# Clustered attention and two expert layers on one core: mask weights and a ranking step one slot later on VectorE, TensorE's slot in another order

## The chip, the cores and the metric

The kernel runs on one core of one Trainium2 chip, as one program with one launch. The metric is the device time of the whole program in microseconds (us), lower is better. The core has five engines that run their own instruction streams and wait for one another by semaphores: TensorE (PE, matmuls and transposes), VectorE (DVE), ScalarE (ACT), GpSimd (POOL) and SyncE (SP, which issues the DMAs here).

## The reference

Three layers follow one another. Only the first is touched by the change:

```python
q_assign = np.argmax(np.einsum('bhsd,hcd->bhsc', q_n, c_n), axis=-1)
k_assign = np.argmax(np.einsum('bhsd,hcd->bhsc', k_n, c_n), axis=-1)
mask = q_assign[:, :, :, None] == k_assign[:, :, None, :]
scores = scale * np.matmul(q, k.transpose(0, 1, 3, 2))
scores = np.where(mask, scores, -1000000000.0)
scores = scores - np.max(scores, axis=-1, keepdims=True)
attn = np.exp(scores)
attn = attn / (np.sum(attn, axis=-1, keepdims=True) + 1e-09)
return np.matmul(attn, v)
```

q, k and v have 2 batches, 8 heads, 768 tokens and 64 values per head; each head has 16 cluster centres, and a query sees only the keys of its own cluster. The result goes through a layer with a rational function between two matrices (512 to 2048 to 512), and then through a layer of 8 experts with soft slots.

## The kernel before, in words

**Pairs and slots.** Attention works on pairs of heads (the two heads of a pair share the partitions), 8 pairs in all. Each pair is cut into 12 slots, so that there are 96 slots, and one loop (L692) runs over slots n. In slot n the *second pass* of slot n and the *first pass* of slot n + 10 are done (`LEAD`, L125). Below, k is n modulo 12, the place of a slot in its pair; a number in brackets is n itself.

- The first pass (`a1_mm`, L375, matmuls L383 and L384) makes the scores of 128 queries against 768 keys in PSUM. VectorE negates them and takes the minimum (`a1_neg`, L393); ScalarE takes the exponent and its sum (`a1_exp`, L401). This gives each query's largest score and sum.
- `stats` (L403) turns these into a logarithm (ACT, L409 and L410), splits it into three bf16 parts on GpSimd (L419 to L432, six steps `parts`), transposes the parts on TensorE (`rows`, L437) and puts them as extra rows under q (`place`, DVE, L444).
- The second pass (`a2_mm`, L451, matmuls L458 and L459) makes the scores with keys on the partitions and the logarithm already taken off; ScalarE takes the exponent (`a2_exp`, L463); the product with v (`a2_av`, L465, matmuls L472) adds up six slots in one PSUM bank, which ScalarE copies out (`copy`, L483) after the sixth, and GpSimd splits (`split`, L492 and L493).

**Buffers that matter.** The scores of both passes take turns in two PSUM tiles (`psS`, tag `S`, L114): within a slot the second pass has one and the first pass the other. There is one PSUM bank for the product with v, three for the small work (`m_tile`, L167), two tiles each for `neg` and `e`.

**Preparation.** `prep(p)` (L236) lists what is to be done for a later pair, three pairs ahead: each step has an offset from the slot in which the list is added (k = 8), an engine and a function. Its steps are cluster scores on TensorE (L251), scaled on ACT (L256), transposed (L266), the best cluster (`best`, DVE, L274 and L275), the first of equal clusters by a rank (`first(0)` L283, `first(1)` L285, `first(2)` L288), the one-hot rows transposed (L293) and counted (ACT, L296), `masks` (DVE, L302, L303, L304: which clusters have a key, then the tile `W` of mask weights), `nonhot` (PE, L309, which reads `W`), `signed` (ACT, L314; the second one issues four DMAs from SP), `alive` (PE, L322), `qalive` (DVE, L326), `ksplit` and `qsplit` (GpSimd, L260, L261, L333 to L335). By their offsets `first(0)` runs at k = 1, `masks` and both `nonhot` at k = 6, `signed` at k = 7 and k = 8. Pair 1 takes its slots from the tuple `PREP1` (L127), and pair 0 is prepared ahead of the loop.

**Decoding.** 32 tiles of 64-bit weights are turned into fp32 beside attention (`decode_steps`, L551): two bit operations on DVE (`bits`, L563 and L564), an exponent on ACT (L567), the mantissa and the sign on DVE (L570, L574), a product and a split on GpSimd (L579, L586, L587), and for half of them transposes and a small product on TensorE (`wphi_steps`, L601, L610, L622). A tile starts every third slot, from slot 72 on every second.

**What sets the order.** TensorE, ScalarE, VectorE and GpSimd run in the order in which the loop calls them (`manual_schedule`, L675); SP's order is left to the framework's planner. The dictionary `plan` holds for each slot and engine the steps that are due; `run(n, ...)` (L663) issues them: at the start of a slot those of SP, ACT, DVE (`D0`, `D`, `D1`, `D2`) and GpSimd, and those of TensorE (`"P"`, the small work) where the loop says so. A slot of TensorE is thus, in this order:

```python
if 0 <= n < NSL:
    a2_mm(p, k)                # second pass of slot n
    a2_exp(p, k)
if n > 0:
    a2_av(pp, pk)              # product with v of slot n - 1
if pend:
    a1_exp(*pend)              # ACT, first pass of slot n - 1
if n + LEAD < NSL:
    a1_mm(*pend)               # first pass, slot n + 10
    a1_neg(*pend)
run(n, "P")                    # small work
```

ScalarE's slot is its planned steps, `a2_exp(n)`, after every sixth product the copy, then `a1_exp` of the slot before. VectorE's slot is its planned steps and then `a1_neg`.

**After attention** the two expert layers run (L753 on); no line of them is changed.

Of the kernel before, what the change touches and what calls it, by code (L numbers as in the profile page):

```python
# [62 lines left out]
def tile_kernel(ctx, tc, qT, kT, v, cenT, cenP, consts, constsb, ab, w_in, w_out, phi, w1, w2, out, dbg=None):  # L63
# [60 lines left out]

    LEAD = 10  # L125

    PREP1 = (-9, -9, -8, -10, -7, -7, -10, -7, -6, -5, -5, -4, -4, -3, -2, -1, 0, 1, -1, 0, 1, 2, -1, 0, 2, 3)  # L127

    OPENW = 4
    ops = [[{n: att.tile([128, S], F32R, name=f"{n}_{i}_{h}") for n in ("q1", "q2", "k1", "k2")}  # L130
# [41 lines left out]
    def first_pair(r, o, f):  # L172

        hold = f["hold"]

        def nonhot_k(h):
            m = psS.tile([128, 2, 512], F32, tag="S", name="s1")
            for c in range(2):
                PE.matmul(m[64:80, c, 0:HS], hold["W"][:, 288 + 16 * h:304 + 16 * h],
                          hold["oT"][:, c * HS:(c + 1) * HS], start=True, stop=True)  # L180
            ACT.activation(o[h]["k2"][64:80, :].rearrange("p (c n) -> p c n", c=2), m[64:80, :, 0:HS], AF.Copy, scale=-BIG)

        def nonhot_q(h, c):
            m = m_tile()
            w = slice(c * HS, (c + 1) * HS)
            PE.matmul(m[64:80, 0:HS], hold["W"][:, 256 + 16 * h:272 + 16 * h], hold["oT"][:, w], start=True, stop=True)
            ACT.copy(o[h]["q2"][64:80, w], m[64:80, 0:HS])

        def q0(h):
            w = slice(0, HS)  # L190
            q1, q2 = o[h]["q1"], o[h]["q2"]
            qa = hold.pop(("qa", h, 0))
            ACT.copy(q1[:, w], qa)
            POOL.tensor_scalar(q2[0:64, w], qa[0:64, :], 1.0, 1.0, ALU.mult, ALU.mult)
            DVE.tensor_tensor(q1[64:128, w], qa[64:128, :], q1[64:128, w].bitcast(F32), ALU.subtract)

        def front():
            f["scores"](0)
            f["scores"](1)
            for h in range(2):  # L200
                f["ksplit"](h)
            idle(2)
            f["scaled"](0)
            f["scT"](0)
            f["best"](0)
            f["scaled"](1)
            f["scT"](1)
            f["best"](1)
            for i in range(3):
                f["first"](i)  # L210
            idle(12)
            f["ohT"]()
            f["count"]()
            idle(8)
            f["masks"]()

        def back():
            f["alive"](0, 0)
            f["alive"](1, 0)
            f["qalive"](0, 0)  # L220
            f["qalive"](1, 0)
            nonhot_k(0)
            q0(0)
            nonhot_q(0, 0)
            q0(1)
            nonhot_k(1)
            nonhot_q(1, 0)
            idle(4)

        rest = [(0, "P", lambda: (f["alive"](0, 1), f["alive"](1, 1))),  # L230
                (1, "D", lambda: (f["qalive"](0, 1), f["qalive"](1, 1))),
                (1, "G", lambda: (f["qsplit"](0, 1), f["qsplit"](1, 1))),
                (1, "P", lambda: (nonhot_q(0, 1), nonhot_q(1, 1)))]
        return front, back, rest

    def prep(p):  # L236
# [4 lines left out]
        hold = {}  # L241
        order = [r["q", 0], r["q", 1], r["k", 0], r["k", 1]]

        def tile_(pool, tag, shape, dt):
            hold[tag] = pool.tile(shape, dt, tag=tag, name=tag)
            return hold[tag]
# [52 lines left out]
        def masks():  # L299

            pres = tile_(s2_p, "pres", [64, 1], F32)
            DVE.memset(pres, 0.0)  # L302
            DVE.tensor_scalar(pres[0:32, :], hold["cnt"][32:64, :], 1.0, None, ALU.min)  # L303
            DVE.scalar_tensor_tensor(tile_(s2_p, "W", [64, B_ADD - B_MASK], BF16), cb[0:64, B_MASK:B_ADD], pres,  # L304
                                     cb[0:64, B_ADD:B_RANK], ALU.mult, ALU.add)

        def nonhot(c):
            m = hold["m", c] = m_tile()
            PE.matmul(m[0:64, 0:HS], hold["W"][:, 256:320], hold["oT"][:, c * HS:(c + 1) * HS], start=True, stop=True)  # L309
# [27 lines left out]
        if p == 0:  # L337
# [6 lines left out]
            (4, "A", lambda: scaled(1)),  # L344
            (4, "D0", lambda: best(0)),
            (4, "P", lambda: scT(1)),
            (5, "D0", lambda: (best(1), first(0))),
            (4, "G", lambda: ksplit(0)),
            (6, "D0", lambda: first(1)),
            (7, "D0", lambda: first(2)),  # L350
            (7, "G", lambda: ksplit(1)),
            (7, "P", ohT),
            (8, "A", count),
            (10, "D0", masks),
            (10, "P", lambda: nonhot(0)),
            (11, "A", lambda: signed(0)),
            (10, "P", lambda: nonhot(1)),
            (12, "A", lambda: signed(1)),
            (12, "P", lambda: alive(0, 0)),
            (13, "P", lambda: alive(1, 0)),  # L360
# [295 lines left out]
    NSL = 12 * NP  # L656
# [35 lines left out]
    for n in range(-LEAD, NSL + 1):  # L692
        p, k = divmod(n, 12)
# [21 lines left out]
        if 0 <= n < NSL:  # L715
            a2_mm(p, k)
            a2_exp(p, k)
        if n > 0:
            pp, pk = divmod(n - 1, 12)
            a2_av(pp, pk)  # L720
            if pk % 6 == 5:
                copy, split = a2_x(pp, pk // 6)
                copy()
                if n < NSL:
                    add(n + (1 if k else 2), [(0, "G", split)])
                else:
                    split()
        if pend:
            a1_exp(*pend)
            pend = None  # L730
        if n + LEAD < NSL:
# [4 lines left out]
            if n < 0:  # L736

                a1_mm(*divmod(n + 1 + LEAD, 12))
        run(n, "P")
        if n < -1:  # L740
            idle(2)
    DVE.tensor_scalar(ncoef, coef, -1.0, None, ALU.mult)
# [448 lines left out]
```

## Time and profile before

| what | value |
|---|---|
| median of 3 runs | 597.94 us (597.42 to 599.94) |
| profiled execution, its own time | 601.37 us |
| its span, first to last instruction | 599.6 us |
| granted TensorE clock over the span | 0.989 |
| attention's slots, and what is left | about 43 to 337 us, 337 to 600 us |
| one pair of heads in the middle of attention | 38.97 us, 12 slots |
| busy PE, DVE, ACT, POOL | 93%, 78%, 66%, 63% |

The profile is of one execution. Times in it are us from the first instruction. The page gives busy shares for the whole span; the trace behind it gives each instruction with its start, its duration and, in square brackets, how long its engine stood idle before it and what ended that. A matmul's printed duration overlaps with the next one's, so that the cost of a group on TensorE is read from starts: from its first start to the first start of what follows.

### The profile page before, as it was taken

Reading aid. Unit: us, or ns where it says so; the run is one execution under the profiler, and the core shown is the slowest. Engines: PE = TensorE matmul, PEld = TensorE weight load, DVE = VectorE, ACT = ScalarE, POOL = GpSimd, SP = SyncE. Lnnn points to the kernel's source line nnn. Section 1 sums busy time; section 2 is a strip of 40 time slices with the busy share of each in tenths; the row PEclk is TensorE's granted clock in tenths of the full one; section 3 lists DMA queues with packets and bytes.
Section 4 is the critical chain, followed back from the end, with each engine's and each line's share of the span. In section 5 each row is a group of like instructions: output and inputs, shape, how many; then the busy total and the mean of one; then the engine's idle time right before and its main releaser. Section 6 shows DMA issues by size and latency. Waiting matters only on the chain.

```text
span 599.6 us, 9906 instructions
## 1 busy us (share of the span) xinstructions
PE 557.7 (93%) x3343; PEld 344.6 (57%) x3346; DVE 468.7 (78%) x817; ACT 393.2 (66%) x713; POOL 377.4 (63%) x487
## 2 busy tenths in 40 slices
PE   8899999999989999999899989999999999978995
PEld 3465555565555655555555667776667757753363
DVE  5779788798787987988984299999899998962033
ACT  3667777787677776787686487777578767740111
POOL 8749899697996988979658365565366545611000
PEclk9989999999999999999999999999999999989999
DMA  8613563354424633244343366766477547379996
GB/s 225 230 37 116 163 192 138 110 181 159 168 89 165 200 117 123 75 137 150 125 157 125 126 224 227 266 210 215 154 270 231 197 164 276 94 293 366 420 419 257
DMA packets 37906, 113.77 MB, mean 190 GB/s; under 512 B 5216, under 2 KB 5664, under 8 KB 33248
## 3 DMA queue, kind: packets, MB, share of 16 engines
q1 hardware_dynamic: 37856, 113.14, 54.1%
q8 instruction: 26, 0.43, 0.3%
q14 instruction: 24, 0.20, 0.1%
HBM read 96.02 MB, written 15.73 MB: 186 GB/s over the span
## 4 chain that ended last, share of the span: by engine, by line
PE 47%; DVE 26%; ACT 10%; POOL 8%; issue 7%; DMA 1%; SPq 0%; DVEq 0%; POOLq 0%; ACTq 0%
DVE neg L393 5%; PE s L383 5%; PE av L472 4%; PE s L458 4%; PE h L809 3%; PE h L812 3%; PE h L810 3%; PE s L384 3%; DVE p L859 3%; PE s L459 3%; PE pb L1042 3%; PE pb L1113 2%; DVE mh L564 2%; ACT neg L401 2%; DVE p L858 2%
## 5 line engine op out<-in xcount | busy, mean ns | idle before, releaser
L393 DVE TENSOR_SCALAR_CACHE_REDUCE neg<-s 128x768 f32<-128x768 f32 x96 | 91.3, 951 | 38.3 <-ACT neg L401 26.1
L463 ACT ACTIVATE e<-s 128x768 f32<-128x768 f32 x96 | 77.5, 807 | 58.3 <-PE s L459 58.2
L401 ACT ACTIVATE neg<-neg,nv 128x768 f32<-128x768 f32 x96 | 89.4, 932 | 9.2 <-DVE neg L393 8.9
L383 PE MATMUL s<-k,q 128*128 128x384 f32 x192 | 76.5, 398 | 13.3 <-DVE neg L393 9.5
L840 POOL TENSOR_SCALAR q<-u,babs 128x512 f32<-128x512 f32 x47 | 40.3, 858 | 75.9 <-ACT u L838 75.9
L472 PE MATMUL av<-e,vt 128*64 128x384 f32 x384 | 83.2, 512 | 0.2 <-ACT e L463 0.2
L809 PE MATMUL h<-xh,w 128*128 128x512 f32 x192 | 80.7, 420 | 0.0
L383 PEld LDWEIGHTS s<-k,q 128*128 128x128 f32 x192 | 36.6, 191 | 68.3 <-DVE neg L393 26.8
L810 PE MATMUL h<-xl,w 128*128 128x512 f32 x192 | 75.9, 395 | 0.0
L458 PE MATMUL s<-q,k 128*128 128x384 f32 x192 | 73.1, 381 | 0.7 <-DVE neg L393 0.5
L842 POOL TENSOR_TENSOR q<-q,u 128x512 f32<-128x512 f32 x47 | 63.8, 1357 | 3.9
L384 PE MATMUL s<-k,q 80*128 80x384 f32 x192 | 65.5, 341 | 0.0
L459 PE MATMUL s<-q,k 128*128 128x384 f32 x192 | 64.7, 337 | 0.0
L812 PE MATMUL h<-xh,w 128*128 128x512 f32 x192 | 52.7, 396 | 0.0
L579 POOL TENSOR_TENSOR w<-mh,ex 128x512 f32<-128x512 f32 x32 | 44.3, 1383 | 10.6 <-DMA w_out<-w 5.3
L859 DVE SCALAR_TENSOR_TENSOR p<-q,p 128x512 f32<-128x512 f32 (+1 forms) x49 | 49.2, 1005 | 0.1
L849 ACT ACTIVATE r<-q,epsc 128x512 f32<-128x512 f32 (+1 forms) x49 | 33.5, 684 | 21.9 <-POOL q L842 20.6
L838 ACT ACTIVATE u<-h 128x512 f32<-128x512 f32 x47 | 27.8, 591 | 27.7 <-PE h L812 27.7
L809 PEld LDWEIGHTS h<-xh,w 128*128 128x128 f32 x192 | 36.2, 189 | 16.9 <-issue 10.3
L458 PEld LDWEIGHTS s<-q,k 128*128 128x128 f32 x192 | 36.0, 188 | 16.2 <-issue 8.3
L841 DVE TENSOR_TENSOR p<-p,h 128x512 f32<-128x512 f32 x47 | 31.8, 677 | 16.9 <-ACT p L839 16.8
L812 PEld LDWEIGHTS h<-xh,w 128*128 128x128 f32 x192 | 36.3, 189 | 8.9
(193 smaller groups left out, 1219.3 us busy)
## 6 DMA issues: line engine op xcount, KB each, us to landing
wt<-w SPq DMA_DIRECT2D x32, 1024.0 KB, 8.0
w<-w_in SPq DMA_DIRECT2D x96, 256.0 KB, 3.1
raw<-w_in SPq DMA_DIRECT2D x16, 512.0 KB, 3.6
raw<-w_out SPq DMA_DIRECT2D x16, 512.0 KB, 3.4
w_in<-w SPq DMA_DIRECT2D x16, 512.0 KB, 2.7
rawk<-kT SPq DMA_DIRECT2D x14, 384.0 KB, 4.0
rawq<-qT SPq DMA_DIRECT2D x14, 384.0 KB, 3.6
w_out<-w SPq DMA_DIRECT2D x16, 256.0 KB, 3.3
```

Source lines behind the costliest of these rows:

```text
L383: PE.matmul(ps[:, c, 0:HS], o["q1"][:, it], o["k1"][:, w], start=True, stop=False)
L384: PE.matmul(ps[:, c, 0:HS], o["q2"][0:80, it], o["k2"][0:80, w], start=False, stop=True)
L393: DVE.tensor_scalar(neg, s1s.pop((p, idx))[:, :, 0:HS], -1.0, None, ALU.mult, ALU.min, accum_out=nvs[p, half][0][:, 0, col:col + 1])
L401: ACT.activation(neg, neg, AF.Exp, scale=-1.0, bias=nv[:, 0, col:col + 1], accum_out=ssum[:, col:col + 1])
L458: PE.matmul(ps[:, h, 0:HS], o["k1"][:, jt], o["q1"][:, w], start=True, stop=False)
L459: PE.matmul(ps[:, h, 0:HS], o["k2"][:, jt], o["q2"][:, w], start=False, stop=True)
L463: ACT.activation(e, s2s.pop((p, k))[:, :, 0:HS], AF.Exp)
L472: PE.matmul(a[64 * h:64 * h + 64, 0:HS], vs[p][:, h, j, :], e[:, h, :], start=(j == 0), stop=(j == 5))
L809: PE.matmul(h, wh[:, c, :], xh[t][:, c, :], start=(c == 0), stop=False)
L810: PE.matmul(h, wh[:, c, :], xl[t][:, c, :], start=False, stop=False)
L812: PE.matmul(h, wl[:, c, :], xh[t][:, c, :], start=False, stop=(c == NCC - 1))
L859: DVE.scalar_tensor_tensor(p[:, w], q[:, w], 2.0, p[:, w], ALU.subtract, ALU.mult)
```

## The change

The step `masks` is cut in two: the memset and the minimum stay at offset 10, and the operation that makes `W` becomes a step `weights` at offset 11 (k = 7). Both `nonhot` move from offset 10 to 11 (k = 7), the first `signed` from 11 to 12 (k = 8). `first(0)` moves from offset 5 to 6 (k = 1 to k = 2), into one step with `first(1)`. `PREP1` gets one more entry, so that pair 1 has masks and weights in the same slot. In the loop the product with v, with the copy and the split that follow it, goes from behind the second pass to the end of the slot.

```diff
-    PREP1 = (-9, -9, -8, -10, -7, -7, -10, -7, -6, -5, -5, -4, -4, -3, -2, -1, 0, 1, -1, 0, 1, 2, -1, 0, 2, 3)
+    PREP1 = (-9, -9, -8, -10, -7, -7, -10, -7, -6, -5, -5, -5, -4, -4, -3, -2, -1, 0, 1, -1, 0, 1, 2, -1, 0, 2, 3)
...
             f["masks"]()
+            f["weights"]()
...
             DVE.tensor_scalar(pres[0:32, :], hold["cnt"][32:64, :], 1.0, None, ALU.min)
+
+        def weights():
+            pres = hold["pres"]
             DVE.scalar_tensor_tensor(tile_(s2_p, "W", [64, B_ADD - B_MASK], BF16), cb[0:64, B_MASK:B_ADD], pres,
                                      cb[0:64, B_ADD:B_RANK], ALU.mult, ALU.add)
...
-            (5, "D0", lambda: (best(1), first(0))),
+            (5, "D0", lambda: best(1)),
             (4, "G", lambda: ksplit(0)),
-            (6, "D0", lambda: first(1)),
+            (6, "D0", lambda: (first(0), first(1))),
...
             (10, "D0", masks),
-            (10, "P", lambda: nonhot(0)),
-            (11, "A", lambda: signed(0)),
-            (10, "P", lambda: nonhot(1)),
+            (11, "D0", weights),
+            (11, "P", lambda: nonhot(0)),
+            (12, "A", lambda: signed(0)),
+            (11, "P", lambda: nonhot(1)),
             (12, "A", lambda: signed(1)),
...
             a2_mm(p, k)
             a2_exp(p, k)
+        if pend:
+            a1_exp(*pend)
+            pend = None
+        if n + LEAD < NSL:
+            pend = divmod(n + LEAD, 12)
+            if n > 0 or n == -LEAD:
+                a1_mm(*pend)
+            a1_neg(*pend)
+            if n < 0:
+
+                a1_mm(*divmod(n + 1 + LEAD, 12))
+        run(n, "P")
         if n > 0:
+
             pp, pk = divmod(n - 1, 12)
             a2_av(pp, pk)
...
-        if pend:
-            a1_exp(*pend)
...
-        run(n, "P")
```

## Rows read from the trace of the kernel before

**Rows 1.** The page, its first part: engines over the whole span.
```profile
PE 557.7 (93%) x3343; PEld 344.6 (57%) x3346; DVE 468.7 (78%) x817; ACT 393.2 (66%) x713; POOL 377.4 (63%) x487
```
**Rows 2.** Windows (length, then busy PE, PEld, DVE, ACT, POOL): a pair; attention's end.
```profile
197.71:236.70 38.99, 37.36 (x214) 21.82 (x211) 33.00 (x62) 29.30 (x55) 33.46 (x49) 1.00 0.43 148
273.40:310.00 36.60, 33.33 (x189) 20.67 (x188) 33.85 (x57) 27.84 (x50) 26.05 (x39) 1.00 0.42 146
```
**Rows 3.** Timeline of PE, slots k = 4 to 6: start, duration, instruction, idle before.
```profile
212.13 0.45 PE L383 MATMUL s<-k,q 128*128 128x384 f32 x1
...
213.04 0.28 PE L437 MATMUL mb<-cb,stat 128*32 128x128 bf16 x2
213.25 0.44 PE L458 MATMUL s<-q,k 128*128 128x384 f32 x1
...
214.15 0.87 PE L472 MATMUL av<-e,vt 128*64 128x384 f32 x4
214.95 0.45 PE L383 MATMUL s<-k,q 128*128 128x384 f32 x1
...
215.76 0.34 PE L458 MATMUL s<-q,k 128*128 128x384 f32 x1
...
216.56 0.87 PE L472 MATMUL av<-e,vt 128*64 128x384 f32 x4
```
**Rows 4.** Timeline of GpSimd, one pair: the logarithm's parts, first and last step.
```profile
186.69 0.20 POOL L419 TENSOR_SCALAR s<-ssum 128x6 f32<-128x6 f32 x1 [3.38 <-ACT neg L401]
...
211.52 0.59 POOL L432 TENSOR_TENSOR stat<-r,stat 128x12 bf16<-128x12 f32 x1
...
225.69 0.20 POOL L419 TENSOR_SCALAR s<-ssum 128x6 f32<-128x6 f32 x1 [2.50 <-ACT neg L401]
```
**Rows 5.** Timeline of PE, the waits at k = 2, 6 and 7.
```profile
205.68 0.44 PE L383 MATMUL s<-k,q 128*128 128x384 f32 x1 [0.65 <-DVE neg L393]
...
218.83 0.51 PE L309 MATMUL mf<-oT,W 64*64 64x384 bf16 x2 [0.22 <-DVE W L304]
...
221.47 0.45 PE L383 MATMUL s<-k,q 128*128 128x384 f32 x1 [0.44 <-DVE neg L393]
222.29 0.60 PE L601 MATMUL mf<-cst,w 128*128 128x128 f32 x4
222.65 0.42 PE L458 MATMUL s<-q,k 128*128 128x384 f32 x1
```
**Rows 6.** Timeline of VectorE, k = 1 and 2, then k = 6 and 7.
```profile
202.14 0.36 DVE L283 TENSOR_TENSOR eq<-eq,cb 128x384 bf16<-128x384 bf16 x1
202.42 2.33 DVE L570 SCALAR_TENSOR_TENSOR mh<-raw,mh 128x512 f32<-128x512 uint32 x1
...
211.33 0.68 DVE L570 SCALAR_TENSOR_TENSOR mh<-raw,mh 128x512 f32<-128x512 uint32 x1
...
217.82 0.95 DVE L304 SCALAR_TENSOR_TENSOR W<-cb,pres 64x320 bf16<-64x320 bf16 x1
218.70 0.41 DVE L563 TENSOR_SCALAR ex<-raw 128x512 int32<-128x512 int32 x1
219.04 1.50 DVE L564 TENSOR_SCALAR mh<-raw 128x512 int32<-128x512 int32 x1
220.46 0.94 DVE L393 TENSOR_SCALAR_CACHE_REDUCE neg<-s 128x768 f32<-128x768 f32 x1
```
**Rows 7.** Timeline of GpSimd beside them.
```profile
201.37 0.83 POOL L260 TENSOR_SCALAR k<-rawk 128x768 fp32r<-128x768 f32 x1
202.28 1.92 POOL L261 TENSOR_TENSOR k<-rawk,k 64x768 fp32r<-64x768 f32 x1
...
218.51 1.75 POOL L579 TENSOR_TENSOR w<-mh,ex 128x512 f32<-128x512 f32 x1
```
**Rows 8.** Timeline of ScalarE, last slots with a first pass.
```profile
316.72 0.81 ACT L463 ACTIVATE e<-s 128x768 f32<-128x768 f32 x1 [0.77 <-PE s L459]
...
318.48 0.30 ACT L409 ACTIVATE l<-ssum,epsc 128x6 f32<-128x6 f32 x1
```

More of the change, by code (lines that the diff above doesn't have):

```diff
@@ L717, in tile_kernel @@
             a2_exp(p, k)
[L718 to L727, printed above, removed]
         if pend:
@@ L739, in tile_kernel @@
         run(n, "P")
+        if n > 0:
+            pp, pk = divmod(n - 1, 12)
+            a2_av(pp, pk)
+            if pk % 6 == 5:
+                copy, split = a2_x(pp, pk // 6)
+                copy()
+                if n < NSL:
+                    add(n + (1 if k else 2), [(0, "G", split)])
+                else:
+                    split()
         if n < -1:
```

## The prediction

> **What bounds the kernel now.** I read the page's busy shares first: TensorE is busy 93% of the span, VectorE 78%, GpSimd 63% [rows 1]. That is an average over stages with different limits, so I looked at the windows next. In a pair of heads in the middle of attention (38.99 us) TensorE has 37.36 us of work on record, GpSimd 33.46 and VectorE 33.00; near the end of attention VectorE has 33.85 of 36.60 [rows 2]. So TensorE leads in the middle, but two others are close, and the question is what stops it when it gets faster. The expert layers, after 337 us, are not touched; I let whatever attention gains or loses pass through whole.
>
> The timeline of TensorE shows what a slot costs, from start to start [rows 3]. A first pass between other kinds of matmul takes 0.91 us (212.13 to 213.04), a second pass 0.90 (213.25 to 214.15), the product with v 0.80. Where there is no small work, a first pass is followed directly by a second pass, and then they take 0.81 (214.95 to 215.76) and 0.80 (215.76 to 216.56): **0.20 us less as neighbours**.
>
> The timeline of GpSimd shows the second limit [rows 4]. At k = 9 its first step on the logarithm's parts waits (2.50 and 3.38 us idle) for ScalarE's exponent; from there GpSimd has work without a gap worth naming until the last of the next half's parts, at k = 4 of the next pair: 186.69 to 212.10, or 25.42 us. TensorE transposes those parts at 213.04 [rows 3], 0.93 us after they are ready. From there to the next k = 9 it is 12.65 us (213.04 to 225.69). So one pair is a **loop**: 25.42 + 0.93 + 12.65 = 39.0 us. It runs five times, from k = 9 of the first pair to k = 9 of the sixth. Only 0.93 us of it is slack.
>
> TensorE's own waits in the pair [rows 5]: at k = 2 the first pass for VectorE (0.65 us), at k = 6 the product for `nonhot` for W (0.22), at k = 7 the first pass again (0.44). That is 1.3 us together. VectorE is late at k = 2 because the mantissa takes 2.33 us, against 0.68 elsewhere, and at k = 7 because W (0.95) and the second bit operation (1.50) lie ahead of the negation, which ends at 221.40 [rows 6]. Both long operations end 0.3 to 0.6 us after a GpSimd operation that was running beside them, at 204.20 and 220.26 [rows 7].
>
> **The change, part by part.**
>
> *The order of TensorE's slot.* No instruction is added. The cycle before is second pass, v, first pass, small work; after it is second pass, first pass, small work, v. So passes are now neighbours in every slot, where before they were so only without small work. Of twelve slots one had none (k = 5). Nine of the other eleven save 0.20; the two that end with transposes of decoded weights save perhaps half, as there the first pass already took 0.82 us (221.47 to 222.29) [rows 5]. That is 9 x 0.20 + 2 x 0.1 = 2.0 us a pair. With the waits gone too, TensorE alone would need 38.99 - 2.0 - 1.3 = 35.7 us.
>
> What moves behind: the product with v itself, whose input is long there (ScalarE's exponent is what the second pass ahead of it also waits for); the copy on ScalarE, now behind `a1_exp`, and GpSimd's split, issued a slot later in any case. The one bank of the product is needed again 2.6 us of passes later, so the copy has cover. The second pass now comes 0.80 us later against the first, and with it ScalarE's exponent and everything queued behind it, the logarithm above all. At k = 9 that is in the loop, and I count it there.
>
> *Weights and `nonhot` a slot later.* One W (0.95) goes from VectorE's k = 6 to k = 7, two small matmuls with it (0.51 together), one `signed` from k = 7 to k = 8 on ScalarE. No DMA changes its slot: the four come with the second `signed`, which stays. GpSimd gets none of it; SP's order is the planner's, which I take as unchanged. What waits for W is `nonhot`, now behind the decode transposes at k = 7, with the product with v and the next second pass queued behind it.
>
> *`first(0)` a slot later.* 0.36 us [rows 6] goes from k = 1 to k = 2. At k = 1 the mantissa could then start at 202.06 instead of 202.42, while GpSimd's earlier operation (201.37 to 202.20) still runs and before the long one starts at 202.28 [rows 7]. Either it stays blocked until 204.20 and nothing changes, or it goes first, VectorE wins up to 1.6 us, and GpSimd's chain grows by up to 0.68, in the loop. Against that stands the last step on the parts, which took 0.59 against 0.20 for the first and could get 0.35 back. I take 0 between -0.35 and +0.68, since GpSimd's phase against VectorE shifts by more than the 0.22 us that decide this.
>
> The Trainium skill, page SBUF — State Buffer, section "Who interferes with whom", says that a VectorE operation with two SBUF inputs and a GpSimd operation that reads SBUF take turns, whoever issues first holding the port for its whole instruction. The trace agrees (2.33 against 0.68 us). By that rule alone the mantissa goes first and each of the five loops grows by about 0.6: 594.7 us instead of the sum below.
>
> *The loop after.* From the transposes at k = 4 to the second pass at k = 8, if nothing waits: small work 0.21, then three times v 0.80 and the joined passes 1.61, then decode transposes 0.36, `nonhot` 0.51, v 0.80: 9.1 us. The second pass there is 0.90; its exponent to the logarithm on ScalarE is 1.76 (316.72 to 318.48) [rows 8]; with 0.1 us of hand-over that makes 11.8 instead of 12.65 us. The wait that can remain is the first pass at k = 7 for the negation of k = 6: by this walk TensorE is there 6.6 us after the transposes. The negation now ends 8.36 us after them (213.04 to 221.40); without W 7.4, and if the second bit operation isn't blocked (0.41, as its neighbour, instead of 1.50) 6.3. So 0 to 0.77 us of wait, and 11.8 to 12.55 us. The slack of 0.93 goes to about 0.05, as TensorE now waits for the parts. **25.42 + 0.05 + 11.8 to 12.55 = 37.3 to 38.0 us, a gain of 1.0 to 1.7 a pair; I take 1.3.**
>
> *Sum.* Five loops: -6.5 us. Before the first pair's k = 9, and from 273 to 310 us, where VectorE is the bound at 92%, I expect little, -0.4 (0 to -1.5). At the end of the first pass's slots the logarithm decides when GpSimd can go on to the last decoded tiles, and it comes later, because the product with v now stands ahead of the second pass whose exponent is queued before it: +0.75 (0 to +0.8). Together -6.2 us. Against the profiled execution's own time that is 601.37 - 6.2 = 595.2; that execution lies 3.4 us above the median of the runs, so against 597.94 it is **591.7 us**. The first pair's and pair 1's edits change places within slots ahead of the loop: nothing either way.
>
> **Rivals.**
>
> - *GpSimd gives it back.* The mantissa goes first at k = 1 (chain +0.68) and the wait at k = 7 is the long one: 26.10 + 0.05 + 12.55 = 38.7, gain 0.3 a pair, and 597.94 - 1.5 + 0.75 = 597.2. For it: slack of 0.93 only [rows 4]. Against it: both ends must fall badly.
> - *The passes don't join.* The first pass waits for VectorE at its first matmul, as it does at k = 2 and k = 7 [rows 5], so its weights aren't ready ahead. Then the walk is about 0.6 us longer, gain 0.7 a pair, or some 595.2 with the tail.
> - *Slower: the first pass at k = 7.* `nonhot` no longer gives cover at k = 6, so TensorE arrives earlier and stands longer. If GpSimd's product runs later and keeps the second bit operation out for another 0.41 us even without W's time being won, the negation ends 8.8 us after the transposes, TensorE waits 2.1 there, and the loop is 26.10 + 0.05 + 13.9 = 40.1: 1.1 worse in five pairs, with the tail 604.2. It decides from about 8.3 us on, which is where the negation ends now; W's 0.95 must be lost again to GpSimd's turns.
> - *TensorE goes free.* If GpSimd's idle time (2.5 us at k = 9) can all be used, the pair falls to about 36 us: 597.94 - 15 + 0.75 = 583.7. Against it: the logarithm's place in the loop.
>
> **How the numbers follow.** About 0.5% (3 us) is what a measurement of this kernel can tell from no change. Forecast 0.49 (own range 588 to 594.9, by 1.7 a pair and -1.5 elsewhere at one end, 0.8 at the other), TensorE free 0.06: faster 0.55. GpSimd gives it back 0.22 and no joining 0.07, both within 3 us of 597.94 by price: same 0.29. Slower 0.16. The range 587 to 600 leaves out TensorE free and most of the slower case, about 0.2.
>
> **What would show it.** A second pass followed by a first pass 0.18 us after its last matmul's start in nearly all slots; a pair of 37.3 to 38.0 us; TensorE's transposes of the parts now waiting for GpSimd at k = 4; no wait for W; the wait at k = 2 smaller; GpSimd's idle time at k = 9 down from 2.5 us by less than a microsecond and a half. Wrong would be: a pair at 39 us or above, with a long wait of the first pass at k = 7, or a pair below 37 with no wait for the parts.

## The result and the profile after

The changed kernel takes 606.65 us (median of 4 runs, 604.78 to 607.56) beside 598.94 us for the kernel before on the same chip (4 runs): ratio **1.0133, 95% interval 1.0111 to 1.0155**. It is slower; 591.7 us was forecast.

The profiled execution took 607.56 us, its span is 605.8. The page, engines over the span and the clock in tenths by slice, answers to [rows 1]:

```profile
PE 554.1 (91%) x3343; PEld 351.1 (58%) x3346; DVE 462.3 (76%) x817; ACT 389.1 (64%) x713; POOL 376.5 (62%) x487
...
PEclk9998998999999899999899999999999999989999
```

The clock row of the kernel before:

```profile
PEclk9989999999999999999999999999999999989999
```

The work is the same, and the shares of PE, DVE, ACT and POOL are lower (that of the weight loads, PEld, is 58% instead of 57%), so time went into standing still. The added time lies in attention: the expert layers' first matmul starts at 343.90 us (337.28 before), and from there to the last matmul of that line it is 185.94 us (185.96 before). The prediction cuts its loop at k = 9, at GpSimd's first step on the logarithm's parts. GpSimd, these steps in the first, sixth and seventh pair, before and then changed:

```profile
69.77 0.20 POOL L419 TENSOR_SCALAR s<-ssum 128x6 f32<-128x6 f32 x1 [1.53 <-ACT neg L401]
...
264.40 0.20 POOL L419 TENSOR_SCALAR s<-ssum 128x6 f32<-128x6 f32 x1 [2.50 <-ACT neg L401]
...
302.07 0.26 POOL L419 TENSOR_SCALAR s<-ssum 128x6 f32<-128x6 f32 x1
```

```profile
71.27 0.20 POOL L424 TENSOR_SCALAR s<-ssum 128x6 f32<-128x6 f32 x1 [4.90 <-ACT neg L406]
...
267.63 0.20 POOL L424 TENSOR_SCALAR s<-ssum 128x6 f32<-128x6 f32 x1 [2.44 <-ACT neg L406]
...
306.44 0.26 POOL L424 TENSOR_SCALAR s<-ssum 128x6 f32<-128x6 f32 x1
```

So the 6.62 us are 1.50 ahead of the first pair's k = 9, 1.73 in the five turns of the loop, 1.14 in the turn behind them, and 2.25 from there to the expert layers, which is called the tail below.

Below, a pair is read from its first product with v to that of the next pair, a turn from k = 9 to k = 9. Windows (length, then busy PE, PEld, DVE, ACT, POOL, then the granted clock): two whole pairs and one short stretch; they answer to [rows 2].

```profile
207.27:245.58 38.31, 35.97 (x212) 22.28 (x211) 31.98 (x62) 28.57 (x55) 31.47 (x48) 1.00 0.39 131
...
87.55:127.59 40.04, 36.89 (x207) 23.01 (x207) 31.68 (x61) 28.30 (x55) 32.87 (x47) 0.96 0.45 148
...
98.15:101.56 3.41, 3.41 (x10) 2.60 (x12) 1.84 (x3) 1.72 (x3) 3.33 (x4) 0.50 0.31 86
```

Two kinds of pair, then. The first has the full clock and is 38.3 us long; the second holds a stretch of 3.41 us in which the granted clock is 0.50, the 1.2 GHz level, and is 40.0 long. Attention has four such stretches (at 53.8, 98.2, 197.1 and 296.1 us); the kernel before had none between its first pair and the expert layers (one lies ahead of them, at 30.3 us).

Timeline of TensorE (start, duration, instruction, idle before), the slots k = 3 and 4 of one pair, then k = 7 and k = 10 of a later one:

```profile
94.26 0.34 PE L463 MATMUL s<-q,k 128*128 128x384 f32 x1
94.44 0.34 PE L464 MATMUL s<-q,k 128*128 128x384 f32 x1
94.61 0.33 PE L388 MATMUL s<-k,q 128*128 128x384 f32 x1
...
97.06 0.29 PE L442 MATMUL mb<-cb,stat 128*32 128x128 bf16 x2 [1.59 <-POOL stat L437]
97.28 0.87 PE L477 MATMUL av<-e,vt 128*64 128x384 f32 x4
98.08 0.64 PE L463 MATMUL s<-q,k 128*128 128x384 f32 x1
98.52 0.52 PE L464 MATMUL s<-q,k 128*128 128x384 f32 x1
98.84 0.52 PE L463 MATMUL s<-q,k 128*128 128x384 f32 x1
99.16 0.52 PE L464 MATMUL s<-q,k 128*128 128x384 f32 x1
...
184.64 0.66 PE L606 MATMUL mf<-cst,w 128*128 128x128 f32 x4 [1.02 <-POOL w L584]
185.23 0.51 PE L313 MATMUL mf<-oT,W 64*64 64x384 bf16 x2
185.67 0.87 PE L477 MATMUL av<-e,vt 128*64 128x384 f32 x4
...
194.73 0.33 PE L326 MATMUL mf<-oT,W 64*128 64x384 bf16 x1
196.17 0.51 PE L252 MATMUL mf<-rawq,cT 64*32 64x384 f32 x2 [1.11 <-ACT sc L257]
```

Four things stand in these rows. The passes did join, in 56 of the 60 slots of pairs 1 to 5: a first pass starts 0.17 us after the second pass's last matmul (94.44 to 94.61), as in the joined slot of [rows 3]. Small work now waits, and behind it stand the product with v and the next second pass: at k = 4 the transposes wait for GpSimd's parts (1.59), at k = 7 the decoded tile's transposes for GpSimd's product of the same slot (1.02), at k = 10 the second cluster scores for ScalarE, which has to free one of the three small PSUM tiles (1.11). In the kernel before these three didn't wait in pairs 1 to 5. Now the first waits in pairs 1, 2, 3 and 5, the second in pairs 2, 3 and 5, the third in pairs 0 to 4; in pairs 1 and 4 it is the first pass that waits at k = 7, for VectorE (0.45 and 0.74). And about 1 us after two of these waits the spacing of the matmuls goes from 0.17 to 0.32 us (98.52, 98.84, 99.16): the low clock. The other two falls of the clock follow waits of the first pass for VectorE, 1.74 us up to 52.83 in pair 0 and 1.53 us up to 294.74.

Timeline of GpSimd, the loop of [rows 4] in one pair, and the product that TensorE awaits at k = 7:

```profile
94.45 0.52 POOL L424 TENSOR_SCALAR s<-ssum 128x6 f32<-128x6 f32 x1
...
96.77 0.24 POOL L437 TENSOR_TENSOR stat<-r,stat 128x12 bf16<-128x12 f32 x1
...
111.29 0.20 POOL L424 TENSOR_SCALAR s<-ssum 128x6 f32<-128x6 f32 x1 [3.58 <-ACT neg L406]
...
182.59 2.00 POOL L584 TENSOR_TENSOR w<-mh,ex 128x512 f32<-128x512 f32 x1
```

From the parts' end (97.01) to the transposes it is now 0.05 us, as predicted. From the transposes (97.06) to GpSimd's next first step (111.29), the prediction's walk from k = 4 to k = 9, it is 14.2 us here, and 13.2 to 13.8 in the pairs after it, where 11.8 to 12.55 was forecast and 12.6 to 13.1 is what the kernel before has. GpSimd stands idle for 3.58 us at the end of it; at the ends of the five turns it is 15.4 us in all, 15.1 before, so no less.

Counted over 44 to 334 us, TensorE waits 0.8 us or more 3 times in the kernel before and **18 times** in the changed one.

### The profile page after: what moved, and what is told of

Its sections match the earlier page's. It is cut to its first block, busy times and chain, and to the rows that moved or that the text cites. A ratio compares the mean times of both kernels' runs of the same rounds, so it can differ in the third digit from the quotient of the medians.

```text
span 605.8 us, 9903 instructions
## 1 busy us (share of the span) xinstructions
PE 554.1 (91%) x3343; PEld 351.1 (58%) x3346; DVE 462.3 (76%) x817; ACT 389.1 (64%) x713; POOL 376.5 (62%) x487
## 4 chain that ended last, share of the span: by engine, by line
PE 54%; DVE 17%; POOL 12%; ACT 8%; issue 6%; DMA 2%; SPq 0%; DVEq 0%; POOLq 0%; ACTq 0%
PE av L477 8%; PE s L463 5%; PE s L388 4%; PE h L815 4%; PE h L818 3%; PE h L816 3%; PE s L464 3%; PE s L389 3%; DVE p L865 3%; PE pb L1048 3%; POOL w L584 2%; DVE p L864 2%; PE pb L1119 2%; ACT e L468 2%; DVE neg L398 2%
## 5 line engine op out<-in xcount | busy, mean ns | idle before, releaser
L477 PE MATMUL av<-e,vt 128*64 128x384 f32 x384 | 85.4, 520 | 0.2 <-ACT e L468 0.2
L388 PE MATMUL s<-k,q 128*128 128x384 f32 x192 | 68.9, 359 | 11.5 <-DVE neg L398 7.6
L463 PE MATMUL s<-q,k 128*128 128x384 f32 x192 | 76.6, 399 | 0.1
L464 PE MATMUL s<-q,k 128*128 128x384 f32 x192 | 66.0, 344 | 0.0
L584 POOL TENSOR_TENSOR w<-mh,ex 128x512 f32<-128x512 f32 x32 | 43.9, 1371 | 11.8 <-DMA w_out<-w 5.3
L388 PEld LDWEIGHTS s<-k,q 128*128 128x128 f32 x192 | 37.2, 194 | 18.7 <-DVE neg L398 11.3
```

Of the source, the lines that this page charges most:

```text
L388: PE.matmul(ps[:, c, 0:HS], o["q1"][:, it], o["k1"][:, w], start=True, stop=False)
L463: PE.matmul(ps[:, h, 0:HS], o["k1"][:, jt], o["q1"][:, w], start=True, stop=False)
L464: PE.matmul(ps[:, h, 0:HS], o["k2"][:, jt], o["q2"][:, w], start=False, stop=True)
L477: PE.matmul(a[64 * h:64 * h + 64, 0:HS], vs[p][:, h, j, :], e[:, h, :], start=(j == 0), stop=(j == 5))
```

## The experiments

The expectations speak of three theories. A: the loop of the prediction stands, and the new order lengthens it because small work with waits of its own now stands in TensorE's path ahead of the product and the next second pass. B: the moved steps do it, through VectorE's and GpSimd's turns. C: the granted clock, which falls after TensorE has stood still, makes a part of the loss of its own. The kernel before ran beside each, with medians of 597.91 to 599.70 us. Where lines are quoted below, they are those of that kernel. The length of a slot is read from the last matmul of its second pass to that of the next slot.

**Which part of the change it is: e1, e2, e14, e15.** e1 is the kernel before with the new order of TensorE's slot alone:

```diff
+        if pend: a1_exp ...; a1_mm ...; a1_neg ...
+        run(n, "P")
         if n > 0: a2_av(pp, pk) ...
-        if pend: a1_exp ...; a1_mm ...; a1_neg ...
-        run(n, "P")
```

> The kernel before with only TensorE's slot in the new order (second pass, first pass, small work, product with v); weights, nonhot and first(0) stay where they were. Theory A (small work now stands ahead of the product with v, so that its waits for GpSimd and ScalarE are no longer filled): nearly the whole loss is here, 603 to 607 us, ratio 1.008 to 1.015, with waits of the small work at k = 4, 7 and 10 and drops of the granted clock in attention. Theory B (weights and nonhot one slot later are the loss, the order by itself is a gain): 590 to 595 us.

606.71 us, 1.0135 (1.0114 to 1.0156), with four stretches at the low clock between 51 and 239 us and 16 waits of 0.8 us or more. The order alone makes the whole loss, but not by the waits of the changed kernel, and the expectation was wrong on two of its three places. TensorE in one pair of e1, k = 2 and k = 6:

```profile
169.41 0.44 PE L383 MATMUL s<-k,q 128*128 128x384 f32 x1 [1.04 <-DVE neg L393]
...
181.38 0.44 PE L383 MATMUL s<-k,q 128*128 128x384 f32 x1 [1.12 <-DVE pres L302]
```

Of the small work only the scores at k = 10 wait long here (1.11), and the transposes at k = 4 and k = 7 don't. Instead the first pass waits for VectorE, at k = 2 (1.0 to 1.95, in three pairs), k = 6 (0.5 to 1.1) and k = 7 (0.4). The five turns are 39.7 to 40.0 us, the three with a low clock in them no longer than the two without. That the two totals agree within 0.1 us doesn't make it one set of waits. e2 is the rest of the change: the changed kernel with the old order.

> The kernel before with only the steps moved (weights, nonhot, signed and first(0) one slot later), TensorE's slot in the old order. Theory A: no loss, 595 to 600 us; the waits for VectorE at k = 2 and k = 7 change by a few tenths. Theory B: 603 to 607 us.

601.24 us, 1.0042 (1.0024 to 1.0059): a loss of its own, which A did not expect, and no part of the sum, for e1 already has it all. The five turns don't show it (194.3 us, 194.6 before). In the profile it lies ahead of the first pair's k = 9 (72.16 us, 69.77 before), where the clock is at 0.50 for 6.8 us instead of 3.4. Timeline of VectorE in e2, then of GpSimd, at k = 1:

```profile
165.33 0.69 DVE L575 SCALAR_TENSOR_TENSOR mh<-raw,mh 128x512 f32<-128x512 uint32 x1
```

```profile
164.66 0.83 POOL L261 TENSOR_SCALAR k<-rawk 128x768 fp32r<-128x768 f32 x1
165.57 2.15 POOL L262 TENSOR_TENSOR k<-rawk,k 64x768 fp32r<-64x768 f32 x1
```

Without the ranking step ahead of it the mantissa starts 0.24 us before GpSimd's long operation and takes 0.69 us, where it took 2.33 [rows 6]; GpSimd's takes 2.15 instead of 1.92 [rows 7], and its chain is 25.92 us instead of 25.41. The wait at k = 2 goes with it (that slot 2.97 us, 3.66 before), but at k = 7 the slot is 4.2 to 4.5 us instead of 3.36, and pairs alternate between 38.05 and 39.6 us. e14 moves only the weights, `nonhot` and the first `signed`, e15 only `first(0)`, in the kernel before; this is the edit of e15:

```diff
-            (5, "D0", lambda: (best(1), first(0))),
+            (5, "D0", lambda: best(1)),
-            (6, "D0", lambda: first(1)),
+            (6, "D0", lambda: (first(0), first(1))),
```

> The kernel before with only the mask weights, nonhot and the first signed a slot later. If the two moved steps cost 0.4% through the wait of the first pass at k = 7 for VectorE (W now stands ahead of the negation there): about 601 us, slot k = 7 at 4.2 us or more against 3.4. If they cost it through the mantissa going first at k = 1: about 598, and slot k = 7 as before.

> The kernel before with only the first ranking step moved from k = 1 to k = 2. If the mantissa goes first and lengthens GpSimd's chain: chain 25.9 us, slot k = 2 at 3.0 instead of 3.6 us, and 600 us or more. If W's move is what costs: about 598 us, the shorter wait at k = 2 paying for the longer chain.

e14: 600.29 us, 1.0042 (1.0027 to 1.0058), slot k = 7 at 4.5 us, turns 0.26 us longer than before. Timeline of VectorE in e14, k = 6 and 7; then of TensorE:

```profile
178.56 0.90 DVE L568 TENSOR_SCALAR ex<-raw 128x512 int32<-128x512 int32 x1
179.37 1.51 DVE L569 TENSOR_SCALAR mh<-raw 128x512 int32<-128x512 int32 x1
180.80 0.95 DVE L398 TENSOR_SCALAR_CACHE_REDUCE neg<-s 128x768 f32<-128x768 f32 x1
...
181.68 1.01 DVE L308 SCALAR_TENSOR_TENSOR W<-cb,pres 64x320 bf16<-64x320 bf16 x1
```

```profile
181.82 0.44 PE L388 MATMUL s<-k,q 128*128 128x384 f32 x1 [0.96 <-DVE neg L398]
```

W is gone from ahead of this negation, and still nothing is won: the first bit operation now takes 0.90 instead of 0.41 us, the second 1.51 as before [rows 6], and TensorE, which no longer stops for `nonhot` at k = 6, is there earlier and stands 0.96 us instead of 0.44 [rows 5]. The expectation had W ahead of the negation; the rows show it behind. e15: 600.09 us, 1.0018 (0.9999 to 1.0037), not clear of no change: the chain is 25.7 us, slot k = 2 is 2.97 in most pairs, and pairs lie anywhere from 37.8 to 40.4 us (the longest has a fall of the clock in it), with waits for the parts (0.52) and, at k = 6, for VectorE's minimum (1.10). Its two runs at a clock of 0.997 and 0.998 took 597.3 and 596.9 us, the eight at 0.987 to 0.992 took 599.5 to 601.5. So e14's step alone costs as much as both together, and that e15's costs anything by itself is not shown. Why the two don't add up in e2 stays open.

**Where v stands: e3, e4.** e3 is the changed kernel, e4 the kernel before, each with the product with v between the first pass and the small work (passes joined, but a wait of small work no longer holds up v):

> The changed kernel with the product with v between the first pass and the small work (second pass, first pass, v, small work): the passes stay neighbours, the small work gets back the 0.8 us of cover ahead of it. Theory A: the waits at k = 7 and k = 10 shrink by about 0.8 us each and the time goes to 592 to 600 us. Theory B: 602 to 607 us.

> The same order (second pass, first pass, v, small work) without the moved steps. Theory A: 592 to 600 us, within 0.5% of the run with the moved steps. Theory B: 588 to 594 us, faster by 1% or more than the run with the moved steps.

e3: 604.02 us, 1.0082 (1.0059 to 1.0105). e4: 609.68 us, 1.019 (1.0139 to 1.0241), five stretches at the low clock in attention. A had 592 to 600 us for both and missed both; B had e3 right by its time and missed e4. Neither does better than the kernel before, and with the old steps this order is the worst of all (at k = 2 the first pass waits 1.75 to 1.97 us in every one of pairs 0 to 5). In e3's profile pairs 0 to 4 are 38.4 to 38.8 us long, a little under the 38.98 of before, with a chain of 26.0 to 26.3. Its ten runs fall apart by the clock: two at 0.995 took 599.7 and 600.0 us, the eight at 0.984 to 0.990 took 602.8 to 605.3.

**Which wait: e5, e6, e7, e9.** All are the changed kernel. e5 takes the wait at k = 7 away by moving the decoded tile's transposes (and what follows, for the tiles begun before slot 72) a slot later, e6 the one at k = 10 by moving the second cluster scores to k = 11, e7 does both, and e9 is e7 with the last two steps of every fourth tile three slots later still:

```diff
-            return [(4, "P", tr), (5, "A", tcopy), ...
+            j = 1 if f < 12 else 0
+            return [(4 + j, "P", tr), (5 + j, "A", tcopy), ...
-            (2, "P", lambda: scores(1)),
+            (3, "P", lambda: scores(1)),
```

> The changed kernel, with the transposes of the decoded w_out tiles and what follows them one slot later (for the tiles begun before slot 72), so that TensorE at k = 7 doesn't wait for the product that GpSimd makes in the same slot. Theory A (the pair is a loop through GpSimd: logarithm's parts, transposes of the parts at k = 4, decoded tile, transposes at k = 7, exponents, next logarithm): the wait at k = 7 goes (1.0 us), the way from k = 4 to k = 9 falls from 13.2 to about 12 us, a pair to about 37.7 us, and the time to 597 to 602 us. Theory C (the clock's drops in attention are nearly all of the loss, and the waits themselves cost nothing): the same number of drops, 604 to 607 us.

> The changed kernel, with the second cluster scores one slot later (k = 11), so that they don't wait at k = 10 for ScalarE to empty the buffer of the first. Theory A: the wait at k = 10 (1.1 us) goes, but it lies beside GpSimd's chain, so a pair without a clock drop stays within 0.3 us of 38.3 to 39.1; the time falls only by what fewer clock drops give, 602 to 607 us. Theory D (the wait at k = 10 is on the path): a pair falls by 1 us, 600 to 602 us.

> The changed kernel with both moves. Theory A: pairs of 37.5 us, no more than one clock drop in attention, 594 to 600 us, so at or below the kernel before. Theory C: as many clock drops as the waits that are left cause; 600 to 604 us.

> The kernel of the two moves (transposes of the decoded tiles and second cluster scores one slot later), with the closing transposes and the sum of every fourth tile three slots later still, since the pairs that hold them took 39.9 us and the others 37.5. Theory A (loop through GpSimd, and VectorE's turns with GpSimd inside it): all pairs 37.3 to 37.8 us, 594 to 597 us at a granted clock of 0.993 or more. Theory C (clock alone): pairs may fall, but waits and with them clock drops stay, 598 to 601 us.

| kernel | us | ratio (95%) | pairs 1 to 4, us | k = 4 to logarithm |
|---|---|---|---|---|
| changed | 606.65 | 1.0133 (1.0111 to 1.0155) | 38.3 to 40.6 | 13.2 to 14.2 |
| e5 | 601.40 | 1.0030 (1.0007 to 1.0052) | 37.2 to 41.2 | 11.5 to 13.9 |
| e6 | 606.77 | 1.0117 (1.0079 to 1.0154) | 39.3 to 40.2 | 13.2 to 14.2 |
| e7 | 599.71 | 1.0013 (0.9988 to 1.0039) | 37.5 and 39.9 in turn | 11.5 and 13.9 |
| e9 | 597.59 | 0.9976 (0.9956 to 0.9997) | 37.5 and 38.0 | 11.5 and 11.9 |

Without the wait at k = 7 the walk comes down to 11.5 us, and the pairs that reach it are 37.2 to 37.5 us long. TensorE and GpSimd in such a pair of e5:

```profile
98.19 0.29 PE L442 MATMUL mb<-cb,stat 128*32 128x128 bf16 x2 [1.06 <-POOL stat L437]
```

```profile
109.68 0.20 POOL L424 TENSOR_SCALAR s<-ssum 128x6 f32<-128x6 f32 x1 [1.15 <-ACT neg L406]
```

In pairs 2 and 4 of e5 and e7, which hold the last two steps of a fourth tile, the walk is 13.9. Without the wait at k = 10 alone nothing is won: it lies beside GpSimd's chain, and slot k = 10 fell from 4.82 to 2.87 us in pairs that didn't get shorter. Windows of e9, two whole pairs, then TensorE's timeline in the second:

```profile
124.74:162.71 37.97, 35.85 (x211) 22.26 (x210) 32.41 (x62) 28.71 (x55) 33.12 (x47) 1.00 0.48 153
162.71:200.21 37.50, 35.42 (x207) 21.79 (x206) 31.28 (x61) 28.64 (x55) 33.40 (x47) 1.00 0.49 158
```

```profile
173.45 0.29 PE L442 MATMUL mb<-cb,stat 128*32 128x128 bf16 x2 [1.27 <-POOL stat L437]
...
180.83 0.51 PE L313 MATMUL mf<-oT,W 64*64 64x384 bf16 x2
...
183.57 0.60 PE L606 MATMUL mf<-cst,w 128*128 128x128 f32 x4
```

The pairs are now those of the prediction, 37.3 to 38.0 us, and the five turns take 187.8 us, 6.8 less than in the kernel before. At k = 7 `nonhot` and at k = 8 the transposes start without a wait. Two waits are left in the loop: the predicted one, for the parts at k = 4 (1.25 to 1.28 us), and ahead of it, at k = 3, one of the first pass for VectorE (0.81 to 0.85). A had 594 to 597 us at a clock of 0.993 or more; the time missed that by little, and the clock of its runs was 0.986 to 0.993.

**The clock: e8, e13.** e8 is the changed kernel with matmuls of zeros ahead of the transposes of the parts (20) and of the scores at k = 10 (18); e13 is e9 with such matmuls ahead of the first pass at k = 3 (14) and of the parts (18). They add zeros to the open sum of the product with v, so that TensorE works where it stood.

```diff
+    def fill_in(c):
+        for _ in range(c):
+            PE.matmul(bank[:, 0:128], nil, identb, start=False, stop=False)
```

> The changed kernel with small matmuls of zeros (they add nothing) put ahead of the transposes of the parts at k = 4 and of the second cluster scores at k = 10, about 1.1 us each, where TensorE waits. All instructions wait as before, TensorE only has work meanwhile. If idle TensorE time at these places lets the clock fall (theory C): drops in attention go from 4 to 0 or 1, granted clock 0.99 or more, 601 to 604 us. If the drops have nothing to do with these waits: clock 0.98, 606 to 609 us.

> The version with the decoded tile's transposes, the second cluster scores and the last steps of the keys' ranking moved to later slots, with matmuls of zeros ahead of the first pass at k = 3 and of the transposes of the parts at k = 4, so that TensorE does not stand still there. Theory C (what is left between 597.6 and the summed 591.7 is the granted clock): no stretch at 0.5 inside attention's pairs, pairs stay at 37.5 to 38.0, clock 0.995 or more, 593 to 595.5 us, clear of the kernel before. Rival: the matmuls of zeros only take the place of the waits and the clock falls elsewhere: 597 to 599 us.

(What this calls the last steps of the keys' ranking are the last two steps of every fourth decoded tile, as in e9.)

e8: 603.18 us, 1.0074 (1.005 to 1.0098). Its windows, two pairs that in the changed kernel were 39.11 and 40.57 us:

```profile
127.62:166.74 39.12, 37.92 (x250) 24.41 (x249) 30.85 (x62) 28.54 (x55) 33.32 (x47) 1.00 0.46 152
166.74:205.71 38.97, 37.49 (x246) 23.94 (x245) 30.73 (x61) 28.43 (x55) 33.16 (x47) 1.00 0.44 149
```

No stretch at the low clock is left in pairs 1 to 7, the six runs have a clock of 0.990 to 0.996 (the changed kernel's four 0.981 to 0.989), and with nothing else changed nearly half the loss is gone. Pairs 1 to 4 are 39.0 to 39.3 us without any fall, as long as before: what the joined passes save goes into waits. The fall of the clock is thus a cost of the waits that comes on top of the waits themselves. e13: 597.63 us, 0.9976 (0.9961 to 0.9992). Its windows, two pairs, and TensorE at k = 4:

```profile
122.11:160.03 37.92, 37.69 (x243) 24.08 (x243) 32.42 (x62) 28.67 (x55) 33.07 (x47) 1.00 0.47 156
160.03:197.50 37.47, 37.22 (x240) 23.57 (x239) 31.32 (x61) 28.62 (x55) 33.39 (x47) 1.00 0.47 156
```

```profile
169.32 1.18 PE L174 MATMUL av<-cb,nil 128*128 128x128 bf16 x18
170.75 0.29 PE L453 MATMUL mb<-cb,stat 128*32 128x128 bf16 x2 [0.25 <-POOL stat L446]
```

Here theory C missed. Attention is free of low clock in the profile, and that execution took 595.79 us at 0.995, close to what was expected; but the median is e9's, as the rival had it, with most runs at 0.990 to 0.993, and pairs 5 to 7 are 1.7 us longer than in e9 (97.3 against 95.7), where the zeros stand in front of work that had no wait. Where the other runs lose their clock isn't on record.

**GpSimd's chain: e10, e11, e12.** The split of the second half of the product moves from k = 2 to k = 8, out of GpSimd's chain into the stretch in which it idles, with a second buffer for its input: e10 in the changed kernel, e11 in the kernel before, e12 in e9.

```diff
-                    add(n + (1 if k else 2), [(0, "G", split)])
+                    add(n + (1 if k else 8), [(0, "G", split)])
```

> The changed kernel, with GpSimd's split of the second half's result (2.6 us) from k = 2, inside the chain from the logarithm to the parts, to k = 8, where GpSimd stands idle; two buffers for x. Theory A: the chain falls from 25.7 to about 23.2 us and the wait for the parts at k = 4 goes; a pair falls by 1 to 2 us to 36.5 to 38 us, and the time to 597 to 602 us. If the pair isn't set by this chain: unchanged, 604 to 607 us.

> The same move of the split in the kernel before. Theory A: there the parts are ready 0.5 to 0.9 us before they are needed and TensorE and VectorE set the pace from k = 9 to k = 4, so the pair stays at 38.5 to 39.0 us and the time within 1.5 us of the kernel before. If GpSimd's chain sets the pair in both kernels: 1 to 2 us less a pair, 590 to 595 us.

> The kernel with all three moves and the split at k = 8. Theory A: nothing of GpSimd's is late, a pair comes near TensorE's own work, 36 to 37 us, and the time to 587 to 594 us, below both kernels. Theory C: the waits that are left keep the clock low and the time at 596 to 600 us.

e10: 605.69 us, 1.0104 (1.0071 to 1.0138); the chain fell to 23.9 to 24.4 us in most pairs, and a wait at k = 7 (slot 4.3; here of the first pass for VectorE, 0.74 to 0.78), the one at k = 10 (4.83) and three falls of the clock, one of twice the length, stayed. That was a miss for A as it stood: the loop through GpSimd isn't the only thing that sets the pair. e12: 600.07 us, 1.0025 (1.0004 to 1.0045), a miss too; with the chain shorter, the first pass waits for VectorE instead, 0.81, 0.46 and 0.77 us at k = 3, 6 and 7 of one pair.

**e11: 596.52 us, 0.9952 (0.9935 to 0.9970), the fastest of all by its median, and faster than both kernels.** A had 38.5 to 39.0 us a pair and a time within 1.5 us of the kernel before, the rival 590 to 595 us; both missed. Its chain is 23.2 us in most pairs with 2.5 to 3.1 us of slack. Timelines of GpSimd, TensorE and VectorE in e11, the slack and k = 6 of a later pair:

```profile
129.67 0.24 POOL L432 TENSOR_TENSOR stat<-r,stat 128x12 bf16<-128x12 f32 x1
```

```profile
133.06 0.29 PE L437 MATMUL mb<-cb,stat 128*32 128x128 bf16 x2
```

```profile
214.77 0.54 DVE L304 SCALAR_TENSOR_TENSOR W<-cb,pres 64x320 bf16<-64x320 bf16 x1
215.24 0.41 DVE L563 TENSOR_SCALAR ex<-raw 128x512 int32<-128x512 int32 x1
215.57 0.62 DVE L564 TENSOR_SCALAR mh<-raw 128x512 int32<-128x512 int32 x1
```

The parts are ready 3.15 us ahead (129.91 to 133.06), so the pair is TensorE's own: 38.1 to 38.6 us instead of 38.98. What shortens it is VectorE at k = 6: with GpSimd's product elsewhere W takes 0.54 instead of 0.95 and the second bit operation 0.62 instead of 1.50 [rows 6], and slot k = 7 goes from 3.36 to 2.85 us. The gain comes by the turns of VectorE and GpSimd, and not by the chain itself, which had 0.49 to 0.93 us of slack already.

## Why the prediction was wrong

**The sum, set against the profile.** For the five turns of the loop −6.5 us was forecast; they came out 1.7 us longer. The three turns without a fall of the clock (39.12, 38.93 and 38.34 us) are 38.80 on the mean, 0.13 shorter than the 38.93 of before instead of 1.3: five times 1.17, or 5.9 us, is the waits. The two with one (40.02 and 39.95) are 1.19 longer than these three: 2.4 us is the clock. That makes the 8.2 us by which the loop missed; the other 4.5 us of the miss are the ends.

*Passes as neighbours.* Right: joined wherever the first pass found its input, and slots without a wait are 2.4 to 2.8 us.

*The chain and its slack.* Right: 25.42 + 0.05 was forecast, 25.5 to 25.9 and 0.05 came (in one pair 0.66). The pair that was read has 0.93 us of slack, its neighbours have 0.49, with a walk of 13.1.

*The walk from k = 4 to k = 9, 9.1 us "if nothing waits".* **This is the step that failed.** The prediction named one wait that could remain, the first pass at k = 7 for the negation. It asked where TensorE would be when, and whether its first pass would find its input, but not the same of the small work, which now stands directly behind the first pass with v and the next second pass in its queue. The decoded tile's transposes need GpSimd's product of their own slot, which ends in mid-slot (184.59); in the order before, a second pass, v and a first pass lay between. The walk was 13.2 us or more: in pairs 2, 3 and 5 by this wait (1.03), in pairs 1 and 4 by the first pass for VectorE (0.45; 0.50 and 0.74), with a fall of the clock in pair 1. It is 11.5 in pairs of e5 and e9, where these transposes come after it; with their 0.36 that is the forecast 11.8. So its arithmetic was right, and what failed is "if nothing waits". e1 shows the same of the order by itself, with a walk of 13.7 to 14.3, by the first pass's waits for VectorE at k = 6 and 7.

*The exponent that comes 0.80 us later.* It was counted at k = 9 only. It also delays `a1_exp` and the scaled scores behind it, and so the PSUM tile that the scores of k = 10 need: 1.11 us in all of pairs 0 to 4. e6 shows that this wait alone costs little in the loop; but of the four falls of the clock the one at 197.1 us follows it.

*The mantissa at k = 1.* 0 was taken between −0.35 and +0.68. e2 decides it: it goes first, and the chain grows by 0.5 (the slack takes it up there, as the turns don't grow). The Trainium skill, page SBUF — State Buffer, section "Who interferes with whom", gave this sign, and these rows agree with the sign (0.69 us for the first comer, 2.15 for the other); it should have been taken.

*The wait at k = 7.* The slower rival's place was right for the steps alone, and e14 has its mechanism (no cover at k = 6, W's time lost again in the bit operations), at 0.3 us a pair instead of 1.1. In the changed kernel the long wait at k = 7 was another instruction's, and the first pass's own was 0.45 and 0.74, in two pairs. That rival's price, 604.2, came nearer than the forecast, but by luck: another cause made it.

*The clock.* The sum had no term for it; every duration was taken at the full clock, since no stretch in the middle of attention before had the lower. This is the second term missed: two falls in the loop (2.4 us), one ahead of it and one behind. e8, which takes only the waits' idle time away, gives back 3.5 us of the median.

*The ends.* −0.4 was forecast for the stretch ahead of the loop and the one behind it, and +0.75 for the tail. They came out +1.50 and +1.14, with a fall of the clock in each, and +2.25. The tail is the order's: it is 37.4 to 37.5 us in the changed kernel, e1, e8 and e9, and 35.2 in the kernel before, e2 and e14. So this term was too small by 1.5 us: the logarithm is 1.0 us later there, as was argued, and what follows it takes 1.3 us more. The upper end of the forecast's own range, 594.9, doesn't follow from its terms as written: 1.0 a pair and +0.8 make 593.7, 0.8 a pair and +0.75 make 594.7.

What stays open: e9 has the loop that was forecast (6.8 us gained), and still ends at 597.6, not 591.7. Part of it shows: ahead of its loop the profile has +2.2 us, with a fall of the clock and a wait of the first pass (1.74) in the first pair, and behind it +2.0, which is its tail. Its runs have a clock of 0.986 to 0.993, in the middle 0.989, those of the kernel before beside it 0.989 to 0.998, in the middle 0.996. Where the clock falls in the executions that weren't profiled is not known, and e13 didn't settle it. Why e1 and the changed kernel come to the same total by waits at different places is not shown.

## What to carry to other kernels

When an in-order queue is put in another order, ask of every instruction in the new place what it waits for and how far its producer has got, not only of the one that was moved, and ask what stands behind it. Ask it of the ends of a loop too: here the tail alone cost 2.25 us. TensorE, busy for 36 of 38 us, lost clock after some waits of 1.1 to 1.7 us, and the low clock took another 1.5 us or so, so a new wait can cost twice its length. Where two engines take turns, a shift of one of them by a few microseconds can be a gain with no work taken away (e11, 0.5%).

## What was not expected of the hardware

**Single waits in a busy stretch were followed by a lower clock.** In the changed kernel TensorE is busy for 36 of 38 us in a pair, and waits of 1.1 to 1.7 us were followed 1.0 to 1.4 us later by 3.41 us at 0.50. In that stretch matmuls start 0.32 us apart instead of 0.175, so 3.41 us do the work of 1.87: 1.5 us each. A wait doesn't always bring it: 18 waits of 0.8 us or more were followed by four falls, e9, which waits 1.25 us or more in each of its pairs 1 to 4, has none there, and the profile of e7 has 16 such waits and none in attention. Nor does a fall always cost that much: in e1 the turns with one are as long as those without. What decides isn't settled.

**The time follows the clock from run to run.** Of the kernel before beside e13, runs at 0.995 and above took 597.3 to 598.7 us and those at 0.992 and 0.993 600.0 to 600.4; the changed kernel's four had 0.981 to 0.989. So a profile's span is read together with its clock.
